# Attention with four query chunks of a head abreast, first maxima by groups of heads, and a two-part output projection

## The chip, the cores and the metric

The kernel runs on one core of a Trainium2 chip. The metric is the time of one execution on the device in microseconds (us). PE is the matrix engine (its weight loads are a row of their own, PEld), ACT the scalar engine, DVE the vector engine, POOL the general engine, SP the engine whose queue issues the DMAs (shown as SPq). The kernel before took 958.94 us, the median of three runs (958.87 to 963.58).

## The reference

Two independent sublayers over 2048 tokens of width 448, their results side by side:

```python
a = jnp.einsum("bsd,ed->bse", x, dft_hid_re)
b = jnp.einsum("bsd,ed->bse", x, dft_hid_im)
y = jnp.einsum("ts,bse->bte", dft_seq_re, a) - jnp.einsum("ts,bse->bte", dft_seq_im, b)
...
scores = jnp.einsum("bhqd,bhkd->bhqk", q, k) * scale
p = _softmax(scores, axis=-1)
o = jnp.einsum("bhqk,bhkd->bhqd", p, v)
```

Half A is a Fourier mixing by matrices. Half B is attention with 16 heads of 28 columns; q, k and v come from one product with `wqkv`, and the heads' outputs go through `wo`. Everything is float32.

## The kernel before, in words

**Number form.** A float32 product is made from rounded parts: a value is split into a rounded high part (ACT copy) and the rest (DVE or POOL subtraction), and high by high, low by high and high by low are summed in a bank of PSUM. A contraction over 448 rows so takes 11 products of 128 rows ("11" in the calls of `products`, L467).

**Filler and attention.** PE's work is of two sorts that are interleaved. The filler (mode 0): the qkv projection (L545), the hidden transforms of half A (also L545) and the two sequence transforms by classes modulo 4 (L800, 768 products of 448 columns). The sequence filler goes in 32 groups of 24 products; each group loads five blocks of DFT matrices, splits or combines them on ACT, DVE and POOL (L787, L789, L758, L763), and DVE reduces each block to a check value (L771).

The attention (L954, `unit_once`) goes in 64 units, one for each head and each chunk of 512 queries. A unit
- multiplies the chunk with the head's first 128 keys (L960), and DVE makes from this the largest score of each query: a transpose in blocks of 32 (L965), a reduction (L966), three copies that bring partition groups beside each other (L970), a reduction (L974), a transpose (L977), and a DMA of the negative maxima as an extra row into the q tile (L979);
- makes 16 score products of 128 keys by 512 queries (L988, 85 rows, "S" below), each followed by an exponential on ACT (L992);
- multiplies all 16 blocks with the values in one burst (L893, "V" below). The values of a block are 128 by 32 (28 columns, a column of ones for the sum, zeros), so a product fills a strip of 32 columns of the array; block kt goes to strip kt % 4, and so four products run side by side. The burst is mode 1: the planner counts a turn from mode 0 to it;
- copies the bank to a tile `ou` (L411 on ACT or L413 on DVE, called from `unit_out`, L897).

The four strips hold partial sums over different keys. `out_of` (L1002) adds them: for a head's four chunks it multiplies the four `ou` tiles with `fold` (L1012), a matrix of four identities, copies the result with ACT (L1015), sends the sums through DRAM to DVE for their reciprocals (L1019, L1020, L1024), spreads them over partitions by DMA (L1028), multiplies on POOL (L1031) and stores to `on_d` (L1034). The last head's four chunks go one by one.

**Output projection** (L1083, `project_out`): after the last chunk's attention, loads `on_d` back, splits it (L1110, L407) and makes 16 results of 11 products (L1129), copied out by ACT or DVE and stored (L1136).

**What sets the order.** All five queues are written out by a planner (L178 to L292) that runs when the program is built. Each task has a key (its due time), engines with assumed durations, what it depends on, and slots of tile pools; the planner walks through assumed time and gives each idle engine the ready task with the lowest key. What it writes out is fixed: on the chip each engine takes its instructions in that order, and a task whose data are late holds all that stands behind it on its engine. Attention keys run from `T_ATT` to `T_END`, filler keys to `T_FILL` (L416).

**Pools.** 16 pairs of tiles `kept` (exponentials, staging), 6 tiles for keys, 3 for queries, 4 `ou`, and 8 banks of PSUM, of which 4 are the filler's and may be borrowed.

**The guard.** Sums of exponentials outside fixed limits (`LIMIT`, `L_LEAST`) or unlike DFT blocks set a flag (L1152 and L1153), and then a second, plain pass (from L1157) does all again. The profiled execution did not run it.

## Time and profile before

| what | us |
|---|---|
| median of three runs | 958.94 |
| the profiled execution's own time | 957.11 |
| its span, first to last instruction | 954.9 |
| busy: PE, ACT, DVE, POOL | 920.9, 695.5, 515.5, 277.3 |

A line such as L988 is a line of the kernel before. In a group of instructions the columns are the line, engine, operation, tiles, shapes, count, then busy time in all and mean ns of one, then the engine's idle time just ahead of them and what ended it. Matrix products are pipelined: one takes longer than the distance to the next, so rates are read from the distance of starts or from the busy time of a whole run of them. A float32 product on a strip (values, `fold`) is recorded as two passes, so 16 products of a burst count as 32. The granted clock (PEclk) is the share of its full clock that PE was given.

### The profile page before, as it was taken

The numbers are of one execution on the slowest core, as the hardware profiler recorded it, in microseconds if no ns is written. First come the engines' busy times: TensorE is split into PE (matmuls) and PEld (weight loads), VectorE is DVE, ScalarE is ACT, GpSimd is POOL, SyncE is SP. The second block draws the span as 40 slices with busy tenths as digits, with TensorE's granted clock in tenths as the row PEclk, the third lists the DMA queues.
The fourth block names the chain that finished last, engine by engine and source line by source line (L and its number), as shares of the span: only waits on it lengthen the run. The fifth ranks groups of instructions, "written<-read, shape, count | busy, mean of one in ns | idle before, by whom it ended". The sixth has DMA issues, their size and how long they took to land. (4 is left out here: it accounts for less than half of the span.)

```text
span 954.9 us, 15430 instructions
## 1 busy us (share of the span) xinstructions
PE 920.9 (96%) x5068; PEld 597.8 (63%) x5068; DVE 515.5 (54%) x1079; ACT 695.5 (73%) x1350; POOL 277.3 (29%) x287
## 2 busy tenths in 40 slices
PE   8999999999999999997999999998899999999896
PEld 6885666665666566664665666564556566665595
DVE  6432232323225222238866776649998686766273
ACT  6167788887778887876888786777797778776541
POOL 1200010231113221115522244236583133314640
PEclk9999999999999999998999999999899999999999
DMA  8992344363335353426554455555638656545853
GB/s 280 209 173 100 114 133 142 110 203 108 121 97 162 91 164 102 154 82 191 154 158 149 117 174 142 147 188 157 213 95 240 188 167 185 170 133 149 233 177 108
DMA packets 188469, 147.54 MB, mean 155 GB/s; under 512 B 52444, under 2 KB 158428, under 8 KB 188380
## 3 DMA queue, kind: packets, MB, share of 16 engines
q1 hardware_dynamic: 188380, 146.46, 51.9%
q8 instruction: 42, 0.69, 0.3%
q14 instruction: 47, 0.39, 0.1%
HBM read 105.12 MB, written 41.03 MB: 153 GB/s over the span
## 5 line engine op out<-in xcount | busy, mean ns | idle before, releaser
L992 ACT ACTIVATE kept<-bank 128x512 f32<-128x512 f32 x1024 | 528.6, 650 | 83.3 <-PE bank L988 77.9
L988 PE MATMUL bank<-q,k 85*128 85x512 f32 x1024 | 352.0, 408 | 7.0 <-DVE ou L413 3.3
L988 PEld LDWEIGHTS bank<-q,k 85*128 85x128 f32 x1024 | 188.5, 190 | 92.7 <-ACT kept L992 29.3
L893 PE MATMUL bank<-kept,v 128*32 128x512 f32 x2048 | 233.5, 595 | 0.2 <-DVE mt L965 0.2
L800 PE MATMUL bank<-big,wlo 128*128 128x448 f32 x512 | 158.6, 380 | 8.7 <-DVE wlo L763 8.5
L893 PEld LDWEIGHTS bank<-kept,v 128*32 128x32 f32 x2048 | 61.7, 109 | 140.5 <-issue 123.6
L763 DVE TENSOR_TENSOR wlo<-wdraw,wraw 128x128 fp32r<-128x128 f32 x188 | 96.0, 549 | 52.1 <-PE bank L800 50.6
L800 PEld LDWEIGHTS bank<-big,wlo 128*128 128x128 f32 x512 | 99.0, 194 | 31.9 <-DVE wlo L763 12.0
L545 PE MATMUL bank<-big,whi 128*128 128x512 f32 (+1 forms) x324 | 109.1, 389 | 2.0 <-DVE big L407 1.4
L965 DVE STREAM_TRANSPOSE mt<-bank 128x512 f32<-128x512 f32 x64 | 45.7, 713 | 120.8 <-PE bank L960 120.6
L411 ACT ACTIVATE ou<-bank 128x512 f32<-128x512 f32 x57 | 34.0, 597 | 94.2 <-PE bank L893 94.1
L800 PE MATMUL bank<-big,whi 128*128 128x448 f32 x256 | 84.7, 373 | 0.8 <-ACT kept L992 0.4
L520 POOL TENSOR_TENSOR wlo<-wraw,whi 128x384 fp32r<-128x384 f32 x22 | 22.8, 1038 | 190.1 <-ACT whi L514 101.3
L789 POOL TENSOR_TENSOR wlo<-wraw,whi 128x512 fp32r<-128x512 f32 x21 | 33.3, 1587 | 150.9 <-PE bank L800 37.0
L545 PEld LDWEIGHTS bank<-big,whi 128*128 128x128 f32 x324 | 60.9, 189 | 21.0 <-issue 6.7
L763 POOL TENSOR_TENSOR wlo<-wdraw,wraw 128x128 fp32r<-128x128 f32 x68 | 50.5, 765 | 62.1 <-PE bank L800 60.0
L771 DVE TENSOR_REDUCE diff<-wlo 128x1 f32<-128x512 f32 x96 | 63.5, 675 | 8.1 <-POOL wlo L758 5.8
L970 DVE COPY mt<-mt 32x16 f32<-32x16 f32 x192 | 60.0, 313 | 3.7
L413 DVE COPY kept<-bank 128x448 f32<-128x448 f32 x37 | 22.3, 617 | 73.3 <-PE bank L545 52.5
L545 PE MATMUL bank<-big,wlo 128*128 128x512 f32 (+1 forms) x160 | 61.9, 388 | 0.0
L758 POOL TENSOR_TENSOR wlo<-wdraw,wraw 128x256 fp32r<-128x256 f32 x44 | 52.7, 1217 | 28.3 <-PE bank L800 26.2
L1031 POOL TENSOR_TENSOR kept<-kept 128x512 f32<-128x512 f32 (+1 forms) x19 | 25.0, 1315 | 122.9 <-DMA kept<-rd 48.2
(95 smaller groups left out, 903.3 us busy)
## 6 DMA issues: line engine op xcount, KB each, us to landing
wdraw<-wre SPq DMA_DIRECT2D x48, 256.0 KB
wdraw<-wim SPq DMA_DIRECT2D x48, 256.0 KB
kept<-abd SPq DMA_DIRECT2D x24, 448.0 KB
qkd<-wd SPq DMA_DIRECT2D x32, 256.0 KB
wraw<-wre SPq DMA_DIRECT2D x32, 256.0 KB
wraw<-wim SPq DMA_DIRECT2D x32, 256.0 KB
k<-qkd SPq DMA_DIRECT2D x64, 112.0 KB
q<-qkd SPq DMA_DIRECT2D x64, 112.0 KB
```

What stands on the lines that cost most here:

```text
L411: nc.scalar.activation(dst, src, AF.Copy)
L545: nc.tensor.matmul(o.t[:, :cols], w(), x(), start=(i == 0), stop=(i == n - 1))
L758: e.tensor_tensor(dst[:, c::2], r[:, c::2], s[:, c::2], op=op)
L763: e.tensor_tensor(dst[:, c], r[:, c], (x if turn % 2 else s)[:, c], op=ALU.subtract if plus else ALU.add)
L771: seen.append(dve(key, lambda: nc.vector.tensor_reduce(dst, f32(src.t).rearrange("p a b -> p (a b)"), axis=AX.X, op=ALU.max, apply_absolut ...
L789: b = both(key - 11.5, lambda e, hi=hi, lo=lo, same=same: e.tensor_tensor(lo.t, classes(same.t), f32(hi.t), op=ALU.subtract), 0.6, 1.25, d ...
L800: nc.tensor.matmul(o.t[:, :D], w.t[:, c], x(), start=first, stop=stop)
L893: nc.tensor.matmul(o.t[j * VW:(j + 1) * VW, :], VT[h].t[:, kt // 4, j, :], pairs[i // 2].t[:, i % 2, :], start=(kt < 4), stop=(kt >= NT - 4))
L965: r = dve(key, lambda: nc.vector.transpose(mt.t[:, :CH], o.t), 0.64, deps=[m], acq=[mt], use=[o], own=RAW_S)
L970: return lambda: nc.vector.tensor_copy(mt.t[:32, CH + i * NT:CH + (i + 1) * NT], mt.t[32 * i:32 * i + 32, CH:CH + NT])
L988: m = pe(key, lambda e, b=b, kt=kt: nc.tensor.matmul(b.t, KT[h][kt // 4].t[:KR + 1, kt % 4 * P:(kt % 4 + 1) * P], q.t[:KR + 1, :], start=T ...
L992: es.append(act(key - 20, lambda b=b, p=p: nc.scalar.activation(p.t, b.t, AF.Exp, scale=SCALE), deps=[m], use=[b, p.pair]))
```

## The change

**Four chunks abreast** (`head_once`, `four`). For heads 0 to 14 the loop over blocks of keys is outside and the four chunks inside: block 0 for chunks 0 to 3, block 1 for chunks 0 to 3, and so on. After 16 scores (four blocks, four chunks) comes a burst of 16 value products in which strip j belongs to chunk j. The strips of the one bank then hold the four chunks' finished sums over all keys; four bursts of a head accumulate into it. There is no copy to `ou` and no product with `fold`: `normal` reads the bank directly. A head now needs all four query tiles at once (8 query tiles in place of 3; 5 key tiles in place of 6). The last head keeps its chunks one by one, with `fold`.

**First maxima of groups of heads** (`tops`). For heads (0, 1), (2 to 5), (6 to 9), (10 to 13), (14, 15) one product for each chunk gives the scores of all heads of the group, by high parts alone, against each head's first 32 keys, laid out as blocks on a diagonal in a tile `kb`. The blocks of 32 make the DVE copies and the second reduction needless: transpose, reduction and transpose remain, once for each group and chunk. The result goes through DRAM (`m_d`) to the query tiles. Queries for these products are loaded extra, through a single tile `qb`.

**Output projection in two parts** (`project_late`). Nine of the eleven products of a result, over `on_d` rows 0 to 383, are filler after the sequence filler; twelve of the sixteen results are copied from their banks to tiles and wait, four stay in the filler's banks. The last two products, over the rows of the last heads, come at the end; DVE adds them to the twelve, and ACT copies the four.

**Planner.** A load marked `hold` isn't issued before the planner's filler front or its time less 60 reaches its key. The assumed flow of DMA goes from 200 to 250, the assumed durations of the sequence filler's block operations are raised, the combining loads' keys move earlier, and the ends of the key ranges move (`T_END` 860 to 783, `T_FILL` 905 to 860, `T_OUT` 860 to 807). The multiplication by reciprocals may go to DVE as well as POOL.

```diff
-NKEYS = 6
+NKEYS = 5
+NQS = 8
+NQB = 1
...
-GV = 16
+GV = 4
...
+GROUPS = ((0, 1), (2, 3, 4, 5), (6, 7, 8, 9), (10, 11, 12, 13), (14, 15))
+FIRST_KEYS = 32
+N_HELD = 12
...
-FLOW, FLOW_IN = 200.0, 400.0
+FLOW, FLOW_IN = 250.0, 400.0
...
+LAG = 60.0
...
+                    if t.hold and t.key > max(front, now - LAG):
+                        aside.append(item)
                         continue
...
+                    front = max(front, t.key) if t.mode == 0 else front
...
-    q_s = new("q", [P, CH], F32R, 3, True)
+    q_s = new("q", [P, CH], F32R, NQS, True)
+    qb_s = new("qb", [P, CH], F32R, NQB, True)
+    kb_s = new("kb", [P, P], F32R, 1)
...
-    ou_s = new("ou", [P, CH], F32, 4, True)
...
-    mt_s = new("mt", [P, CH + 6 * NT], F32, 1)
-    top_s = new("top", [32, 32], F32R, 1)
...
+    top_s = new("top", [P, 32], F32R, 2)
...
-    T_ATT, T_END, T_FILL, T_OUT = 34.0, 860.0, 905.0, 860.0
+    T_ATT, T_END, T_FILL, T_OUT = 34.0, 783.0, 860.0, 807.0
...
+                a = act(key - 12, lambda hi=hi, same=same: nc.scalar.activation(hi.t, classes(same.t), AF.Copy), 1.02,
...
-                        e, j, part, dl.t, r.t, same.t, cross.t), 0.72 if j == 2 else 0.88, 1.44 if j == 2 else 1.7,
+                        e, j, part, dl.t, r.t, same.t, cross.t), 1.1 if j == 2 else 1.45, 2.25 if j == 2 else 2.5,
...
+    def tops(g):
+        hs = GROUPS[g]
+        n = len(hs)
+        at = head_at[hs[0]] - LEAD
+        kb = kb_s.slot()
+        def keys():
+            for i, h in enumerate(hs):
+                r0 = h * 2 * DH + DH
+                nc.sync.dma_start(f32(kb.t)[i * DH:(i + 1) * DH, i * 32:(i + 1) * 32], f32(qk_d[r0:r0 + DH, 0, :FIRST_KEYS]))
+        lk = dma(at - 13, keys, hold=True, size=4, n=n, deps=[d for h in hs for d in rows_ready(h, 0, DH)], use=[kb])
+        for c in range(NC):
+            qb = qb_s.slot()
+
+            def rows(qb=qb, c=c):
+                src = bass.AP(tensor=qk_d.tensor, offset=qk_d.offset + hs[0] * 4 * DH * S + c * CH,
+                              ap=[[4 * DH * S, n], [2 * S, DH], [1, CH]])
+                nc.sync.dma_start(f32(qb.t)[:n * DH], f32(src))
+            lq = dma(at - 12 + c, rows, hold=True, size=56 * n, deps=[d for h in hs for d in rows_ready(h, c, 0)], use=[qb])
+            o, mt, top = bank_s.slot(), kept_s.slot(), top_s.slot()
+            m = pe(at + c, lambda e, o=o, qb=qb: nc.tensor.matmul(o.t[:32 * n], kb.t[:n * DH, :32 * n], qb.t[:n * DH], start=True, stop=True),
+                   deps=[lk, lq], use=[o, qb, kb])
+            key = at + c - 20
+            r = dve(key, lambda o=o, mt=mt: nc.vector.transpose(mt.t[:32 * n, 0], o.t[:32 * n]), 0.64, deps=[m], acq=[mt], use=[o], own=RAW_S)
+            r = dve(key, lambda mt=mt: nc.vector.tensor_reduce(
+                f32r(mt.t[:32 * n, 1, :NT]), mt.t[:32 * n, 0].rearrange("p (j r) -> p j r", r=32), axis=AX.X, op=ALU.max, negate=True), 0.6,
+                deps=[r], use=[mt], own=RAW_S)
+            r = dve(key, lambda mt=mt, top=top: nc.vector.transpose(
+                f32(top.t)[:32 * n], mt.t[:32 * n, 1, :NT].unsqueeze(1).to_broadcast([32 * n, 2, NT])), SMALL, deps=[r], acq=[top], use=[mt])
+            s = dma(key, lambda top=top, c=c: nc.sync.dma_start(m_d[g * NC + c][:32 * n], f32(top.t)[:32 * n]), size=4 * n, deps=[r], use=[top])
+            for i, h in enumerate(hs):
+                top_done[h, c] = s, m_d[g * NC + c][32 * i:32 * i + NT]
+
...
+    def four(h, o, tiles, es, key, kts, cs, after=None):
+
+        def emit(e):
+            for i, (kt, c) in enumerate((kt, c) for kt in kts for c in cs):
+                j = c if len(cs) > 1 else kt % 4
+                nc.tensor.matmul(o.t[j * VW:(j + 1) * VW, :], VT[h].t[:, kt // 4, kt % 4, :], tiles[i // 2].t[:, i % 2, :],
+                                 start=(kt < 4 // len(cs)), stop=(kt >= NT - 4 // len(cs)))
+        return pe(key, emit, d=0.2146 * len(kts) * len(cs), deps=[*es, *got_v[h], after], use=[*tiles, VT[h], o], mode=1)
...
+    def head_once(h):
+        t_b = head_at[h]
+        alone = h == H - 1
+        head_loads(h, [t_b - 12 + c * (4 if alone else NT) * DT for c in range(NC)], t_b - 10)
+        if alone:
+            for c in range(NC):
+                chunk_once(h, c, qs[c], got_q[c], t_b + c * NT * DT)
+            return
         last_pv = None
         for g in range(NT // GV):
+            tiles, es = [], []
+            for i in range(GV * NC):
+                kt, c = GV * g + i // NC, i % NC
+                if i % 2 == 0:
+                    tiles.append(kept_s.slot(SPARE))
+                key = t_b + (kt * NC + c) * DT
+                es.append(score(h, c, kt, qs[c], got_q[c], tiles[-1], i % 2, key))
+            last_pv = four(h, po, tiles, es, key, range(GV * g, GV * (g + 1)), range(NC), last_pv)
+        normal([(h, c) for c in range(NC)], h, po, last_pv, key + 10)
...
+    def normal(us, g, o, dep, key):
+
+        n = len(us)
+        pair = kept_s.slot()
-
-        def emit(e):
-            for i, u in enumerate(us):
-                nc.tensor.matmul(o.t[i * VW:(i + 1) * VW, :], fold, OU[u].t, start=True, stop=True)
-        m = pe(key, emit, d=0.86, deps=[ou_done[u] for u in us], use=[o, *(OU[u] for u in us)], mode=1,
-               wait=JOIN if key < T_END - 30 else 0.0)
         a = act(key - 20, lambda: nc.scalar.activation(
-            osb.t[:n * VW], o.t[:n * VW], AF.Copy, accum_out=sums[:n * VW, g:g + 1]), deps=[m], use=[o, pair])
+            osb.t[:n * VW], o.t[:n * VW], AF.Copy, accum_out=sums[:n * VW, g:g + 1]), deps=[dep], use=[o, pair])
...
-        mul = pool(key - 20, lambda: nc.gpsimd.tensor_tensor(osb.t[:n * VW], osb.t[:n * VW], sbc.t[:n * VW], op=ALU.mult),
+        mul = both(key - 20, lambda e: e.tensor_tensor(osb.t[:n * VW], osb.t[:n * VW], sbc.t[:n * VW], op=ALU.mult), 0.62, POOL_2,
...
-    combine(0, lambda g: s_at - 12 + 6 * g if g else h_at + (s_at - h_at) / QT, lambda g: x_users, lambda g, j: [h_last] if g else x_users)
+    combine(0, lambda g: s_at - 18 + 8 * g if g else h_at + (s_at - h_at) / QT, lambda g: x_users, lambda g, j: [h_last] if g else x_users)
...
+        for cc in range(2):
+            cols = slice(cc * 2 * CH, (cc + 1) * 2 * CH)
+            for k in range(3):
+                raw = kept_s.slot()
+                key = fkey(0, 0) + 2 * cc * 36 * M448 - 14 + k
+                ld = dma(key, lambda raw=raw, k=k, cols=cols: nc.sync.dma_start(
+                    raw.t.rearrange("p a b -> p (a b)"), on_d[k * P:(k + 1) * P, cols]), 512, hold=True,
+                    deps=[o_done[h, c] for h in heads_in(k) for c in (2 * cc, 2 * cc + 1)], use=[raw])
+                for i in range(2):
+                    c = 2 * cc + i
+                    free = u_last[1, c + 1] if c < 3 else z_last[1, 2, 3]
+        held = {}
+        spare = [kept_s.slot() for _ in range((N_HELD - 10 + 1) // 2)]
+        for n in range(NT):
+            c, t = divmod(n, 4)
+            cut = lambda k, c=c, t=t: (lambda: place_of(c, k)[:, t * P:(t + 1) * P])
+            seq = products(cut, lambda k, cut=cut: cut(3 + k), lambda: None, lambda k: (lambda: w.h[:, k]), lambda k: (lambda: w.l[:, k]))[:9]
+            o = fill_s.slot()
+            key = fkey(9, M448)
+            for i, (a, b) in enumerate(seq):
+                def emit(e, i=i, a=a, b=b, o=o, n=n):
+                    nc.tensor.matmul(o.t[:, :D], a(), b(), start=(i == 0), stop=(i == 8 and n < N_HELD))
+                last[0] = pe(key + i * M448, emit, d=M448, deps=[last[0], *x[c, i // 3], *(w_ready if i == 0 else ())], use=[o])
...
+        x3 = [q_s.slot() for _ in range(NC)]
+        x3_ready = []
+        for c in range(NC):
+            raw = kept_s.slot()
...
+        for n in range(NT):
+            c, t = divmod(n, 4)
+            key = T_OUT + n
+            o = bank_s.slot() if n < N_HELD else held[n]
+
+            def emit(e, n=n, o=o, xt=x3[c], t=t):
+                for i, y in enumerate((w.h, w.l)):
+                    nc.tensor.matmul(o.t[:, :D], xt.t[:, t * P:(t + 1) * P], y[:, 3], start=(i == 0 and n < N_HELD), stop=(i == 1))
+            p = pe(key, emit, n=2, d=M448, deps=[x3_ready[c], *w_ready, *([] if n < N_HELD else [last[0]])], use=[o, x3[c]])
+            if n < N_HELD:
+                s, at, put = held[n]
+                e = dve(key, lambda o=o, at=at: nc.vector.tensor_tensor(at(), at(), o.t[:, :D], op=ALU.add), 0.53, deps=[p, put], use=[o, s])
+                dma(key, lambda at=at, n=n: nc.sync.dma_start(out[n * P:(n + 1) * P, D:], at()), deps=[e], use=[s])
+            else:
+                pair = kept_s.slot()
+                e = act(key, lambda o=o, pair=pair: nc.scalar.activation(pair.t[:, 0, :D], o.t[:, :D], AF.Copy), 0.43, deps=[p], use=[o, pair])
+                dma(key, lambda pair=pair, n=n: nc.sync.dma_start(out[n * P:(n + 1) * P, D:], pair.t[:, 0, :D]), deps=[e], use=[pair])
```

More of the change, by code (lines that the diff above doesn't have):

```diff
@@ L139 @@
 class Task:
-    __slots__ = ("engs", "key", "emit", "lat", "use", "lock", "left", "then", "mode", "n", "dmas", "own", "since", "wait")
+    __slots__ = ("engs", "key", "emit", "lat", "use", "lock", "left", "then", "mode", "n", "dmas", "own", "since", "wait", "hold")
 class Schedule:
@@ L187, in run @@
         done = set()
-        landed, flow = [], FLOW_AT
+        landed, flow, front = [], FLOW_AT, 0.0
         while True:
@@ L370, in tile_kernel @@
         nc.gpsimd.memset(f32(k)[64:96, :], 1.0)
+    for k in kb_s.tiles:
+        nc.gpsimd.memset(f32(k), 0.0)
     class Half:
@@ L428, in plan @@
             head_due_b[h] = min(due[h, c][1] for c in range(NC))
-    plan(T_ATT, T_END, LEAD, 0.5)
+    head_at = [T_ATT + h * (T_END - T_ATT) / H for h in range(H)]
+    DT = (T_END - T_ATT) / (H * NC * NT)
     V_PACE = 1.0
@@ new lines, in score @@
+    def score(h, c, kt, q, got, pair, i, key):
+        b = bank_s.slot()
+        p = Half(pair, i)
+        m = pe(key, lambda e: nc.tensor.matmul(
+            b.t, KT[h][kt // 4].t[:KR + 1, kt % 4 * P:(kt % 4 + 1) * P], q.t[:KR + 1, :], start=True, stop=True),
+            deps=[*got, *got_k[h, kt // 4], before.get("rb")], use=[b, pair, q, KT[h][kt // 4]])
+        in_line("rb", m)
+        return act(key - 20, lambda: nc.scalar.activation(p.t, b.t, AF.Exp, scale=SCALE), deps=[m], use=[b, pair])
@@ L1139, in tile_kernel @@
+    for g in range(len(GROUPS)):
+        tops(g)
+    for h in range(H):
+        head_once(h)
     w_out = Weights(big[:, :8 * D])
-    project_out(w_out, load_w(w_out, lambda k: wo[:, k], g_at[1, NQ - 1, 1] - 10, after=[u_last[1, 0]]), T_OUT, [before["rb"]])
+    project_late(w_out, load_w(w_out, lambda k: wo[:, k], g_at[1, NQ - 1, 1] - 10, after=[u_last[1, 0]]))
     r = [dve(T_OUT, lambda: nc.vector.tensor_reduce(alike[:, 0], diff, axis=AX.X, op=ALU.max), 0.2, deps=seen),
```

186 lines of the change are left out of this document (97 added, 89 removed).

## The prediction

> **What bounds the kernel now.** I read the page's busy shares first, then the windows of all engines (columns: window, length, then busy us and count of PE, PEld, DVE, ACT, POOL, then granted clock, DMA share, GB/s).
>
> ```profile
> PE 920.9 (96%) x5068; PEld 597.8 (63%) x5068; DVE 515.5 (54%) x1079; ACT 695.5 (73%) x1350; POOL 277.3 (29%) x287
> ...
> 200.00:300.00 100.00, 100.00 (x568) 61.75 (x567) 27.94 (x73) 79.08 (x158) 15.00 (x18) 1.00 0.42 135
> ...
> 400.00:500.00 100.00, 93.75 (x524) 60.05 (x523) 66.10 (x122) 77.06 (x151) 35.04 (x34) 0.97 0.49 151
> 500.00:600.00 100.00, 97.91 (x568) 61.85 (x567) 70.66 (x141) 77.93 (x148) 32.72 (x31) 1.00 0.50 146
> 600.00:700.00 100.00, 93.43 (x505) 56.26 (x503) 76.50 (x133) 76.52 (x150) 51.85 (x46) 0.97 0.55 167
> 700.00:800.00 100.00, 98.15 (x562) 62.12 (x565) 80.34 (x159) 79.23 (x150) 37.08 (x31) 1.00 0.61 182
> ```
>
> PE sets the time in every stretch after the start. From 200 to 300 it never rests; from 400 on, with the sequence filler, it loses a few us in each hundred, while DVE's load goes from 28 to 80. No other engine is near its end there. So two things can shorten the kernel: fewer products, and fewer waits of PE. The waits, by who ended them (us in all, times, longest), and the slices in which the clock fell (PE alone: busy, clock, DMA share, GB/s):
>
> ```profile
> PE bank L800 <- DVE wlo L763: 8.5, 6, 5.5
> PE bank L988 <- DVE ou L413: 3.3, 1, 3.3
> PE bank L1129 <- POOL big L407: 2.0, 1, 2.0
> PE bank L988 <- DVE mt L965: 1.8, 3, 0.8
> ...
> PE bank L960 <- DMA q<-qkd: 1.8, 1, 1.8
> ...
> PE bank L1129 <- ACT big L498: 1.4, 1, 1.4
> ...
> PE bank L893 <- DVE mt L965: 0.2, 1, 0.2
> ```
>
> ```profile
> 30.00:40.00 10.00, 8.24 (x33) 0.83 0.92 266
> 40.00:50.00 10.00, 10.00 (x50) 1.00 0.98 171
> 50.00:60.00 10.00, 9.54 (x45) 1.00 0.98 166
> ...
> 440.00:450.00 10.00, 3.86 (x12) 0.79 0.92 291
> 450.00:460.00 10.00, 10.00 (x47) 0.87 0.51 146
> ...
> 660.00:670.00 10.00, 8.69 (x47) 0.89 0.21 61
> 670.00:680.00 10.00, 9.84 (x58) 0.94 0.87 279
> 680.00:690.00 10.00, 6.73 (x24) 0.83 0.45 131
> ...
> 900.00:910.00 10.00, 9.95 (x41) 0.84 0.87 245
> ```
>
> DVE ended 8.5 + 3.3 + 1.8 + 0.2 = 13.8 us of PE's waits. The clock took more: 10 x (0.21 + 0.13) = 3.4 us after the gap near 446, 10 x (0.11 + 0.06 + 0.17) = 3.4 after those near 666 and 684. A gap so costs itself and, if it is long enough, 1.7 us or more.
>
> **The change part by part.** I take counts of the changed kernel from its built instruction order.
>
> ```profile
> L988 PE MATMUL bank<-q,k 85*128 85x512 f32 x1024 | 352.0, 408 | 7.0 <-DVE ou L413 3.3 <-DVE mt L965 1.8 <-ACT kept L992 1.8
> L893 PE MATMUL bank<-kept,v 128*32 128x512 f32 x2048 | 233.5, 595 | 0.2 <-DVE mt L965 0.2
> ...
> L970 DVE COPY mt<-mt 32x16 f32<-32x16 f32 x192 | 60.0, 313 | 3.7
> L965 DVE STREAM_TRANSPOSE mt<-bank 128x512 f32<-128x512 f32 x64 | 45.7, 713 | 120.8 <-PE bank L960 120.6
> L966 DVE TENSOR_REDUCE mt<-mt 128x16 f32<-128x512 f32 x64 | 43.6, 681 | 1.7
> ...
> L411 ACT ACTIVATE ou<-bank 128x512 f32<-128x512 f32 x57 | 34.0, 597 | 94.2 <-PE bank L893 94.1
> ...
> L960 PE MATMUL bank<-q,k 84*128 84x512 f32 x64 | 26.0, 406 | 2.2 <-DMA q<-qkd 1.8 <-ACT kept L992 0.5
> ...
> L1012 PE MATMUL bank<-ou,fold 128*32 128x512 f32 x128 | 20.2, 605 | 0.1
> ...
> L974 DVE TENSOR_REDUCE mt<-mt 32x16 fp32r<-32x64 f32 x64 | 16.0, 251 | 2.2
> ...
> L977 DVE STREAM_TRANSPOSE top<-mt 32x32 f32<-32x32 f32 x64 | 12.8, 200 | 2.2
> ...
> 850.00:875.00 25.00, 2.09 (x4) 0.28 (x4) 1.00 0.46 134
> ```
>
> The last row is the window of L1012 alone.
>
> *Folds.* Four passes there, two of the last head's single folds, take 2.09. The changed kernel keeps four such folds, 4.18 us, of 20.2: **-16.0**. They stood on a full PE, so all of it counts.
>
> *First maxima.* 20 products in place of 64. A score product in a run costs the distance of starts: (0.86 - 0.39) / 2 = 0.235 us from the rows
>
> ```profile
> 882.48 0.86 PE L988 MATMUL bank<-q,k 85*128 85x512 f32 x3
> ...
> 884.27 0.39 PE L988 MATMUL bank<-q,k 85*128 85x512 f32 x1
> ...
> 921.31 11.37 PE bank L1129 x55
> ```
>
> 44 x 0.235 = **-10.3** (with the mean of one, 0.406, it would be 17.9; I take the distance, as PE is pipelined).
>
> *Unchanged.* 1024 scores, 64 bursts of 16 value products (233.5 us), 1604 filler and 176 projection products are all still there. The strips are used in turn, 0 to 3, in both; I cost four abreast at nothing.
>
> *DVE and ACT.* A unit's maxima cost DVE 0.713 + 0.681 + 3 x 0.313 + 0.251 + 0.200 = 2.8 us, 178 in all. Now 20 times 0.713 + 0.681 + 0.200, 32 in all: 146 us of DVE go, some 22 of the 66 to 80 in each hundred. ACT loses 53 of its 57 copies to `ou` (32 us); 12 multiplications go from POOL to DVE (0.68 each by the nearest row, L966's 128x512 pass: 8 us). None of this is on PE's path, but it is what stood ahead of the waits that DVE ended. I take those 13.8 and their 6.8 of clock as gone: **-20.6**, bounds 0 and -20.6. Late next is POOL, which shares the filler's blocks.
>
> *Projection.* The products only move: in the built order 118 + 30 of them, not 176 and 57 of filler, follow the last burst. The waits at its start (2.0 + 1.4, clock 10 x 0.16 = 1.6) came from splitting `wo`; that split now has 84 filler products of cover behind its release, not 36. I take half: **-2.5**, bounds 0 and -5.0. Its DMAs, copies and 12 additions lie beside products.
>
> *Start.* Head 0 now needs four query tiles and four `qb` loads before its first burst: 4 x 112 + 2 x 168 KB more, 0.80 MB, where DMA is full (0.98, 166 to 171 GB/s in the rows above): **+4.8**, bounds 0 and 12 (two clock falls and the longer way through DRAM). Behind a waiting top product or score stand the filler products, so it is PE that pays.
>
> *End.* Four stores of 224 KB leave together, not one by one: 0.69 MB at 166 to 291 GB/s, 2.4 to 4.1 us, partly beside the copies: **+2**. The last chunk's way from fold through DRAM to its two products is covered by 112 + 22 products of 11.37 / 55 = 0.207 us, 27.7 us.
>
> ```profile
> 892.74 1.04 PE L1012 MATMUL bank<-ou,fold 128*32 128x512 f32 x2
> ...
> 931.07 0.42 ACT L1110 ACTIVATE k<-kept 128x256 fp32r<-128x256 f32 x1
> ```
>
> ```profile
> L1019 SPq DMA_DIRECT2D sm<-kept x5: 612/622/624, 217.2 to 419.9; - x5
> ```
>
> ```profile
> L1031 POOL TENSOR_TENSOR kept<-kept x4: 1283/1285/1291, 226.9 to 379.7; 128x512 f32<-128x512 f32 x4
> ```
>
> Before it took 38.3 us (892.74 to 931.07), but in a queue full of filler loads; with a quiet queue (from 217.2 to 226.9) the part up to the multiplication takes 9.7. I take 0, bounds 0 and 10.6 + 1.7.
>
> *New waits.* A top product waits for the single `qb`; SP waits with it, and K, Q and matrix loads stand behind SP. The nearest row is the 1.8 us wait of L960, after which the clock fell (10 x 0.17 = 1.7): 3.5 us each. I take one, **+3.5**, bounds 0 and 20 x 3.5.
>
> On the clock the trace and a page differ. The Trainium skill, "TensorE: Matmul & The Clock Gate", Part 1, says that the clock halves after an idle window of about 3.4 us; in this trace it fell after gaps of 1.8 and 3.3 too. By the page alone only the 5.5 us gap of L800 would cost clock, and the sum would be that of rival 5.
>
> Sum: -16.0 - 10.3 - 20.6 - 2.5 + 4.8 + 2 + 3.5 = -39.1. The profiled execution took 957.1 (span 954.9 and 2.2 around it): 918.0. It lies 1.8 below the median of 958.9, so I add that: **920**.
>
> **The rivals.**
> 1. *The waits stay and change their cause.* The order is planned from assumed durations and nothing shows that POOL or DMA can't take DVE's place as releaser. Then 20.6 + 2.5 are not won: 943. Against it: DVE has the waits, and sheds about three tenths of its load.
> 2. *Every wait goes*: no loss at start, end and tops (4.8 + 2 + 3.5), the projection's other 2.5, and PE's waits for exponentials (1.8 and 0.5 in the rows of L988 and L960), ahead of which copies go: 905.
> 3. *The tops hold PE, and it gets slower.* Place: the 20 top products behind one `qb`. Price 3.5 each. Without such waits the sum is 916; 42 us are made up from 12 waiting products on, and with all 20 it is 986. Against it: only one of 64 waited so before, and outside the start DMA is half idle.
> 4. *Four abreast is not side by side.* If strips that hold the same values ran 0.6 us slower a burst (4.2 for 3.6), 64 x 0.6 = 38 us would eat the gain: 958. Against it: the strips' turn is the same.
> 5. *The clock falls only after gaps over 3.4 us.* Then the falls near 666, 684 and 900 came by themselves and stay, 3.4 + 0.8 less won: 924. This is the page's rule; the slices speak against it.
> 6. *The guard trips*, since 32 keys give lower maxima than 128, and the second pass adds its whole time, over 900. From the inputs the largest log of a sum is 54, the limit's is 82.9.
>
> **How the numbers follow.** Forecast 0.52, rivals 0.17, 0.18, 0.05, 0.03, 0.04 and 0.01. The likeliest case gives 920. The range reaches over rival 5, to rival 1 above and a little past rival 2 below: 900 to 943; outside lie rivals 3, 4 and 6 and the edges of 1 and 2, together about 0.2. A measurement of this kernel can tell 0.5% from no change. Faster: forecast and rivals 1, 2, 5, 0.91; the same: rival 4, 0.03; slower: rivals 3 and 6, 0.06.
>
> **What would show it.** Folds: 8 passes, about 4 us. Tops: 20 products. Bursts: 3.6 us each; more is rival 4. DVE's busy time near 385, ACT's near 660. Waits of PE from 430 to the attention's end that DVE ended: near none, clock 1.00; else rival 1, and its releaser names the cause. A wait at top products or the first burst of several us shows the start's or rival 3's price. After the last burst about 148 products, 31 us, with no gap ahead of the last eight. A PE that waits in many places at once would prove the forecast wrong.

## The result and the profile after

The changed kernel takes **994.67 us** (median of 4 runs, 991.42 to 997.25) against 959.74 for the kernel before beside it (958.87 to 963.58). The ratio is 1.0354 with a 95% interval of 1.031 to 1.0399: slower, where 920 was forecast. The profiled execution took 996.12, its span is 994.3. The busy shares of after:

```profile
PE 925.9 (93%) x4904; PEld 593.4 (60%) x4904; DVE 416.6 (42%) x722; ACT 660.6 (66%) x1279; POOL 244.4 (25%) x247
```

The work went as intended: 164 matrix passes fewer, 99 us less of DVE, 35 less of ACT. PE is busy for longer all the same and its share fell from 96% to 93%: it does less, more slowly, and waits more. Where, the windows show. They are cut at the start of head 7's first score product and at the end of the last score product (columns as in the prediction). Before, then after:

```profile
0.00:409.20 409.20, 403.45 (x2223) 263.12 (x2223) 137.99 (x350) 299.84 (x584) 67.67 (x90) 1.00 0.50 145
409.20:886.20 477.00, 460.24 (x2573) 288.34 (x2570) 345.95 (x662) 371.39 (x712) 184.59 (x170) 0.99 0.53 160
886.20:954.90 68.70, 57.21 (x277) 46.38 (x276) 31.54 (x68) 24.28 (x55) 24.99 (x27) 0.95 0.58 176
```

```profile
0.00:438.60 438.60, 410.08 (x2139) 264.88 (x2139) 85.98 (x184) 280.89 (x554) 54.78 (x79) 0.96 0.46 135
438.60:949.50 510.90, 478.40 (x2573) 298.11 (x2572) 317.25 (x513) 369.59 (x707) 189.25 (x168) 0.97 0.57 172
949.50:994.30 44.80, 37.46 (x195) 30.43 (x194) 13.34 (x27) 10.11 (x21) 0.37 (x1) 0.96 0.31 103
```

Heads 0 to 6 take 29.4 us more, heads 7 to 15 33.9 more, the rest 23.9 less. To split this I went through PE's products one by one in each trace. A product's distance to the next start counts as work up to the usual distance of its kind (score 0.236, 512 columns 0.233, 448 columns 0.206, bursts and folds as they run at full clock); the idle time before the next is a gap; half the time at the halved clock is clock. What is left, starts that come later than usual without a gap, is called slow starts; the trace gives no cause for them.

| us, before to after | work | gaps | clock | slow starts | sum |
|---|---|---|---|---|---|
| heads 0 to 6 | 391.3 to 380.9 | 4.4 to 27.2 | 1.7 to 14.1 | 10.5 to 15.1 | +29.3 |
| heads 7 to 15 | 436.0 to 440.1 | 16.8 to 32.5 | 6.1 to 13.2 | 17.9 to 24.9 | +33.9 |
| after the last score | 54.2 to 37.3 | 3.5 to 0.0 | 1.7 to 0.0 | 1.2 to 0.1 | -23.2 |
| all | -23.2 | +35.0 | +17.8 | +10.5 | +40.1 |

So 23 us of work were saved and 63 lost around it. What PE waited for in after (us, times, longest):

```profile
PE bank L984 <- DMA qb<-qkd: 30.3, 10, 6.1
PE bank L1000 <- ACT kept L1004: 8.6, 11, 2.0
PE bank L1000 <- DMA q<-md: 3.8, 4, 1.8
PE bank L815 <- DVE wlo L778: 3.2, 4, 0.8
PE bank L1011 <- DMA v<-vd: 2.8, 1, 2.8
```

Half of all gaps stand ahead of the product of the grouped first maxima (L984) and end when its query rows land in `qb`. Before, transfers ended 1.8 us of PE's waits. Five of these ten waits, 18.8 us, lie in heads 0 to 6, the other five, 11.5 us, in heads 7 to 15. The longest stands ahead of the very first of the 20 products, whose load is issued at 27.82 into an empty `qb`:

```profile
33.09 0.66 PE L984 MATMUL bank<-qb,kb 56*64 56x512 f32 x1 [6.11 <-DMA qb<-qkd]
```

Another wait in full, first SP's queue, then PE (start, us, what; in brackets the idle time before it), then SP's own waits for the store of the maxima from 155 to 190:

```profile
160.90 0.37 SPq L993 DMA_DIRECT2D md<-top  x1
165.81 0.24 SPq L1036 DMA_DIRECT2D q<-md  x1
166.13 0.68 SPq L981 DMA_DIRECT2D qb<-qkd  x1
...
172.58 0.23 SPq L1036 DMA_DIRECT2D q<-md  x1
173.32 0.67 SPq L981 DMA_DIRECT2D qb<-qkd  x1
```

```profile
163.39 0.50 PE L984 MATMUL bank<-qb,kb 112*128 112x512 f32 x1
...
165.60 1.83 PE L1000 MATMUL bank<-q,k 85*128 85x512 f32 x7
172.53 0.77 PE L984 MATMUL bank<-qb,kb 112*128 112x512 f32 x1 [5.09 <-DMA qb<-qkd]
173.09 1.05 PE L1000 MATMUL bank<-q,k 85*128 85x512 f32 x2
```

```profile
SPq L1036 <- DMA md<-top: 8.9, 3, 4.5
```

The product at 163.39 frees the one `qb`. The next load could go then, but SP's queue first holds the read of the stored maxima, which waits until their store (160.90) has landed, at 165.81. Only at 166.13 is the load of `qb` issued, and 6.4 us later, at 172.53, the next product can run. All that stands behind it on PE waits along. Two products then take 1.05 us instead of 0.6: the clock has fallen. It fell after shorter gaps too. Here a gap of 1.96 stands ahead of a burst that takes 5.34 us; the burst at 159.82 took 3.64:

```profile
159.82 3.64 PE L1011 MATMUL bank<-kept,v 128*32 128x512 f32 x32
```

```profile
372.53 0.51 PE L984 MATMUL bank<-qb,kb 112*128 112x512 f32 x1 [1.96 <-DMA qb<-qkd]
372.97 5.34 PE L1011 MATMUL bank<-kept,v 128*32 128x512 f32 x32
```

The windows around it, with the granted clock in the third column from the end:

```profile
369.65:373.06 3.41, 1.45 (x9) 0.58 (x11) 0.62 (x1) 2.35 (x5) 1.45 (x2) 1.00 0.60 213
373.06:376.47 3.41, 3.41 (x20) 0.87 (x24) 1.61 (x3) 0.00 (x0) 0.00 (x0) 0.50 0.40 101
376.47:379.88 3.41, 3.41 (x27) 1.49 (x19) 0.40 (x1) 1.10 (x3) 0.00 (x0) 1.00 0.23 77
```

The trace has 13 stretches at half clock, before had 6; six of the 13 begin during or just after a wait for `qb`, 34.1 us long in all, which costs 17 us at most.

### The profile page after: what moved, and what is told of

Same layout as the page of the kernel before. It is cut to its first block, busy times and chain, and to the rows that moved or that the text cites. A ratio compares the mean times of both kernels' runs of the same rounds, so it can differ in the third digit from the quotient of the medians.

```text
span 994.3 us, 14609 instructions
## 1 busy us (share of the span) xinstructions
PE 925.9 (93%) x4904; PEld 593.4 (60%) x4904; DVE 416.6 (42%) x722; ACT 660.6 (66%) x1279; POOL 244.4 (25%) x247
## 5 line engine op out<-in xcount | busy, mean ns | idle before, releaser
L1000 PE MATMUL bank<-q,k 85*128 85x512 f32 x1024 | 362.5, 416 | 16.1 <-ACT kept L1004 8.6
L1011 PE MATMUL bank<-kept,v 128*32 128x512 f32 x2048 | 238.8, 608 | 2.8 <-DMA v<-vd 2.8
L778 DVE TENSOR_TENSOR wlo<-wdraw,wraw 128x128 fp32r<-128x128 f32 x188 | 105.2, 596 | 62.6 <-PE bank L815 49.8
L560 PE MATMUL bank<-big,whi 128*128 128x512 f32 (+1 forms) x324 | 113.2, 400 | 2.4 <-ACT big L497 1.4
L535 POOL TENSOR_TENSOR wlo<-wraw,whi 128x384 fp32r<-128x384 f32 x22 | 23.2, 1055 | 305.6 <-ACT whi L529 170.6
L815 PE MATMUL bank<-big,whi 128*128 128x448 f32 x256 | 89.4, 391 | 1.3 <-DVE kept L427 1.3
L560 PEld LDWEIGHTS bank<-big,whi 128*128 128x128 f32 x324 | 62.4, 196 | 22.3 <-issue 6.3
L778 POOL TENSOR_TENSOR wlo<-wdraw,wraw 128x128 fp32r<-128x128 f32 x68 | 55.1, 836 | 76.2 <-DMA wdraw<-wre 39.4
L802 ACT ACTIVATE whi<-wraw 128x512 fp32r<-128x512 f32 x32 | 37.8, 1189 | 41.2 <-DMA wraw<-wim 19.2
L815 PEld LDWEIGHTS bank<-big,whi 128*128 128x128 f32 x256 | 50.6, 202 | 13.3 <-issue 4.2
L602 DVE TENSOR_TENSOR wd<-bank,wd 128x512 fp32r<-128x512 f32 x16 | 10.9, 686 | 98.3 <-ACT wd L601 98.3
L560 PE MATMUL bank<-wd,big 128*128 128x448 f32 x176 | 40.5, 387 | 0.1
```

The costliest lines, as they stand in the source:

```text
L535: b = sch.add(e, at, lambda g: eng[g].tensor_tensor(self.lo.t[:, :n], raw.t[:, :n], f32(self.hi.t)[:, :n], op=ALU.subtract), deps=[a], acq ...
L560: nc.tensor.matmul(o.t[:, :cols], w(), x(), start=(i == 0), stop=(i == n - 1))
L778: e.tensor_tensor(dst[:, c], r[:, c], (x if turn % 2 else s)[:, c], op=ALU.subtract if plus else ALU.add)
L802: a = act(key - 12, lambda hi=hi, same=same: nc.scalar.activation(hi.t, classes(same.t), AF.Copy), 1.02, deps=[raws[0][1]], acq=[hi], use= ...
L815: nc.tensor.matmul(o.t[:, :D], w.t[:, c], x(), start=first, stop=stop)
L1000: m = pe(key, lambda e: nc.tensor.matmul(b.t, KT[h][kt // 4].t[:KR + 1, kt % 4 * P:(kt % 4 + 1) * P], q.t[:KR + 1, :], start=True, stop=True),
```

## The experiments

Theory A: the grouped maxima hold PE, by the single `qb` and the way through DRAM and back. Rival B: the written order is at fault as a whole, and a wait taken away returns with another cause. Rival C: four chunks abreast want too much at a head's start. Rival D: the planner's new numbers (rate, durations, pacing). These letters hold for my own text; an expectation says itself what its letters stand for (in e3_owntops B is four abreast, in e4_projout C is the split projection). All but the last two kernels were timed once. One kernel's times lie up to 14 us apart (w2_lead18: 942.4 to 956.1; h2_lat and w1_lat, the same kernel: 956.7, and 952.0 to 961.2), so I read where the time goes and not only the end. Beside them the kernel before took 961.3 (e), 956.6 (f), 957.4 (g) and 959.5 (h).

**e1_extra.** `tops`, the load of `qb`, in the planner's list only:
```diff
-... size=56 * n, deps=...
+... size=56 * n, extra=3.0, deps=...
```


> Only the planner is told 3 us more for each query load of a top product; the chip's work is the same. Theory A (top products stand in PE's order ahead of loads that take 5 to 6 us through one qb tile and hold everything behind them: 30.3 us of waits and 18.7 us of clock at those places): PE's waits for qb fall from 30 to under 5 us, clock over 0.98, time 944 to 960. Rival B (the waits only show what is short anyway, so they come back at scores or sequence filler): waits of PE stay over 55 us in all, time 980 or more.

992.48 us. The waits for `qb` fell from 30.3 to 6.7, yet gaps only from 59.7 to 46.4, slow starts rose from 40.1 to 47.0. A's numbers were missed. B's time held; its 55 us of waits did not quite.

**e2_nqb2.**
```diff
-NQS = 8
-NQB = 1
+NQS = 7
+NQB = 2
```


> Two qb tiles (and 7 query tiles in place of 8, for room). Theory A: a load no longer waits for the product before it, so the second to fourth product of a group wait less; the planner still assumes short loads, so some waits stay: PE's waits for qb 5 to 15 us, time 952 to 972. Rival B: 980 or more. If one query tile less hurts, it shows as waits of scores for q.

967.58 us, as A said: 27 won by one more buffer. `qb` waits 12.0, gaps 39.4; heads 0 to 6 fell from 438.6 to 420.5. So the buffer is the larger part, and not all: the wait for the first load is still 6.2 long.

**e3_owntops.** Four abreast and the split projection stay; each chunk takes its maxima from its own rows and 128 keys, as before (`tops` gone; the product, transpose, reductions and store of the old `unit_once` in its place).

> Four abreast and the split projection stay, but every chunk makes its first maxima by itself from 128 keys, as before: 64 top products, no qb, no way through DRAM. Theory A: the 49 us of waits and clock go, 44 products of 0.235 come back, DVE is as full as before: time 945 to 970. Rival B (four abreast itself, with its new order and plan, is what loses): 980 or more.

985.02 us, which missed A's number and lies in its B's 980 or more. But heads 0 to 6 take 414.0 here; the loss is in heads 7 to 15, 521.3 (before 477.0).

**e4_projout.** `project_out` at the end in place of `project_late`.

> The output projection is one part at the end again, the rest of the change stays. Theory A: the split isn't the loss and is worth some us of filler under the attention: 996 to 1012. Rival C (the split holds the end back, by its loads and held results): under 988.

1015.34 us, above its A's 996 to 1012 and far from its C. The rest after the last score takes 94.4 instead of 44.8, heads 7 to 15 493.7 instead of 510.9, the time up to head 7 425.4 instead of 438.6: beside this plan the split wins 50 at the end and costs 30 ahead of it. The plan's pacing is made for a split, though: it costs 28 after the last score without one (h4_beforepace). Against the kernel before e4 so says nothing of the split.
```profile
425.40:919.10 493.70, 468.74 (x2495) 287.44 (x2495) 276.68 (x451) 362.60 (x695) 150.87 (x132) 0.95 0.52 156
```

**f1_latency.** e2_nqb2 and in the planner's list
```diff
-the load of qb: size=56 * n          +size=56 * n, extra=3.0
-the store of the maxima: size=4 * n  +size=4 * n, extra=1.5
-their load into q: size=2            +size=2, extra=1.5
```


> The kernel after with two buffers for the grouped q rows (as in e2_nqb2, 967.6 us) and, in the list that the planner orders by, a longer landing for the three transfers of the first maxima: 3.0 us more for the q rows, 1.5 us more for the store of the maxima and 1.5 us more for their load into q. If the waits for these three legs are what is left of the loss (12.0 us at the top products, and the head's start), 948 to 960 us with under 4 us of qb waits. If a wait that is taken away only comes back with another cause, as in e1_extra, 962 us or more with gaps still near 40 us.

966.59 us, as rival B would have it: waits for `qb` 8.7, not under 4, and 6.2 now for the maxima.

**f2_flow.** `FLOW` 250 to 200.

> The kernel after with the planner's assumed rate of transfers set back from 250 to 200, nothing else. If that assumption lets the plan start products before their rows have landed, 960 to 980 us. If it is not the cause, 985 to 1005 us, and the difference from 992 shows how far any new order of the same work scatters.

1013.49 us, above both bands. The old rate doesn't take the loss away, and another order of the same work can cost 19 us more. So a single step of that size, or smaller, can come from the order alone.

**f3_beforeplan.** The kernel before with `FLOW` 250 and the longer durations of the block splits.

> The kernel before with the planner's new figures alone (rate 250, and the longer durations of the splits of the sequence blocks), the work unchanged. If the figures make a worse order by themselves, 970 us or more. If not, 950 to 966 us.

965.55 us, 9 above before, inside the band for "not". D's numbers alone explain little.

**f4_onebyone.** Head's chunks one after the other, folds as before, grouped maxima and split projection kept (`NQS` 4, four `ou` tiles):
```diff
-        if alone:
-            for c in range(NC):
-                chunk_once(h, c, qs[c], got_q[c], t_b + c * NT * DT)
-            return
+        for c in range(NC):
+            chunk_once(h, c, qs[c], got_q[c], t_b + c * NT * DT)
+        if not alone:
+            out_of([(h, c) for c in range(NC)], h, t_b + NC * NT * DT + 10)
```


> The kernel after with the chunks of each head one after the other again (16-product bursts into one chunk, folds as before), while the first maxima stay in groups of four heads over one buffer and the projection stays split. If taking four chunks abreast is what brings the loss, because a head then needs all four q rows and maxima at its start, 945 to 970 us (the folds cost 12 more). If the grouped maxima behind one buffer bring it, 985 us or more with qb waits of 25 us or more.

995.11 us, and its first row of waits:
```profile
PE bank L984 <- DMA qb<-qkd: 29.5, 11, 5.7
```
Without four abreast the loss and the waits are those of after. Four abreast isn't needed for it: C falls as the main cause.

**g1_firstown.** e2_nqb2, with own maxima for heads 0 and 1 only (`range(1, len(GROUPS))`).

> The kernel after with two buffers for the grouped q rows (e2_nqb2, 967.6 us), and heads 0 and 1 taking their first maxima from their own q rows and 128 keys as in the kernel before, so that the first group has no store of maxima and no second trip through DRAM; the other four groups unchanged. If the start's loss (head 0 takes 113.5 us in e2_nqb2 against 100.0 before and 103.7 with own maxima everywhere) is that extra trip, 952 to 960 us. If it is the opening of head 0 with four chunks at once, 964 us or more.

961.06 us, between the two. Heads 0 to 6 414.7, from 420.5.

**g2_onebyone2.** f4_onebyone with `NQB` 2 and `NQS` 3.

> f4_onebyone (chunks one after the other, grouped maxima, split projection; 995.1 us) with two buffers for the grouped q rows (and three for q instead of four). If the single buffer is what holds the top products, 960 to 975 us, as it was worth 27 to the kernel after. If the groups cost in some other way, 985 us or more.

979.40 us, between the two: 16 won, waits for `qb` 15.5 from 29.5. The buffer is about half of the waits.

**g3_projonly.** The split projection with the planner's changes, without the other two parts: f4_onebyone with own maxima as in e3_owntops.

> The split projection alone: chunks one after the other, each chunk's first maxima from its own q rows and 128 keys, folds as before, with the planner's new figures. If the grouped maxima bring the loss, and four abreast on top of own maxima brings its own (e3_owntops, 985.0 us), this is 935 to 955 us, faster than the kernel before by what the projection gives (some 15 to 20 us). If the split projection or the planner's figures bring the loss, 970 us or more.

980.54 us, far over the 935 to 955 of A and in the other side's 970 or more. Its windows, cut as above:
```profile
0.00:408.60 408.60, 401.98 (x2205) 264.60 (x2205) 132.33 (x348) 296.74 (x579) 61.52 (x85) 1.00 0.47 138
408.60:931.40 522.80, 489.59 (x2658) 307.13 (x2657) 375.33 (x715) 386.91 (x735) 198.63 (x184) 0.95 0.55 166
```
Up to head 7 nothing is lost against before (409.2). Heads 7 to 15 take 46 more: 16.4 of work (folds and own maxima kept, filler and projection moved in from the end), 16.4 of gaps, 12.8 of clock. The releasers and, in slices of 10 us, the places where PE lost most:
```profile
PE bank L816 <- DVE wlo L779: 12.3, 12, 2.1
PE bank L1024 <- ACT kept L1028: 9.1, 5, 5.9
PE bank L816 <- DVE wlo L805: 7.3, 2, 7.0
```
```profile
470.00:480.00 10.00, 3.42 (x19) 1.62 (x12) 9.91 (x12) 5.64 (x12) 7.54 (x7) 0.81 0.67 193
...
680.00:690.00 10.00, 7.95 (x18) 5.26 (x18) 9.95 (x13) 5.89 (x12) 5.61 (x5) 0.55 0.88 286
...
900.00:910.00 10.00, 3.36 (x14) 2.48 (x14) 9.97 (x11) 4.35 (x8) 7.46 (x7) 0.81 0.47 134
```
DVE is full there, 9.9 of 10, though over the span it is busy for little more than half. These are the places where a class of the sequence starts (`combine` beside the block splits) and the end of the blocks. In the kernel before DVE was as full at such places: 9.93 from 440 to 450, 9.99 from 670 to 680.

**g4_projonly_oldplan.** g3_projonly with f3's numbers set back.

> g3_projonly with the planner's rate (200) and the durations of the sequence blocks' splits as in the kernel before. If those figures cost what they cost alone in f3_beforeplan (9 us), 928 to 945 us; if they make no order of this work better or worse by themselves, within 8 us of g3_projonly either way.

984.49 us: within 8 of g3. D's rate and durations don't explain g3.

**h3_projpace, h4_beforepace.** `T_END, T_FILL, T_OUT`: g3_projonly with 860, 905, 860; the kernel before with 783, 860, 807 and `s_at - 18 + 8 * g`.

> g3_projonly (split projection alone, 980.5 us) with the planner's pacing as in the kernel before (attention to end at 860 and the sequence products at 905 instead of 783 and 860). g3 loses nothing up to head 7 and then 45 us in heads 7 to 15. If the new pacing is what crowds VectorE and GpSimd there, 940 to 960 us. If the split projection itself does (its loads, splits and stores lie in those heads), 970 us or more.

> The kernel before with the pacing of the kernel after alone (783, 860, 807, and the first combination's keys), the work unchanged. If the pacing makes the loss of the second half, 975 us or more, with the loss in heads 7 to 15 and none before. If not, 950 to 968 us.

973.30 and 981.76 us. With the old pacing g3's heads 7 to 15 still take 516.8, inside the band for the split itself. But the stretch now holds 37 matrix passes more (2695 for 2658), and PE's waits in it fall from 33.1 to 22.2: a part of g3's loss there is the pacing. On the kernel before the new pacing does cost 22, as its number said, but not where I expected it. The window of h3, then those of h4:
```profile
416.40:933.20 516.80, 494.54 (x2695) 315.69 (x2695) 375.26 (x714) 388.85 (x740) 204.35 (x187) 0.96 0.55 167
```
```profile
400.40:883.10 482.70, 467.97 (x2577) 289.09 (x2576) 321.41 (x619) 374.29 (x716) 185.60 (x181) 0.97 0.51 154
883.10:980.00 96.90, 75.43 (x336) 60.50 (x334) 52.21 (x100) 25.62 (x54) 37.25 (x39) 0.84 0.55 175
```
Heads 7 to 15 take 5.7 more than before, the rest 28.2 more: 59 more matrix passes are put off past the attention, and the clock there is 0.84. The new pacing goes with a long end in both kernels that have the projection whole, this one and e4_projout; with it split it won nothing either (g3 980.54, h3 973.30).

**h2_lat, h1_pace.** g1_firstown with f1's three landings; and that with the pacing 820, 900, 842.

> g1_firstown (961.1 us) with the three longer landings of f1_latency in the planner's list. Those took away nearly the whole wait at head 5 and changed nothing in heads 7 to 15, so 953 to 960 us if the remaining group waits (7.5 us) go; 961 us or more if they come back elsewhere.

> h2_lat with another pacing (820, 900, 842). If the second half's loss comes with the crowding that the pacing sets, 940 to 952 us, faster than the kernel before; if it is only another order of the same work, 950 to 975 us.

956.66 and 961.48 us, both inside their bands (h1's for another order of the same work). h2_lat reaches head 7 at 410.8 (g1 414.7); the group wait at head 5 is gone. The other pacing gives nothing.

**w1_lat, w2_lead18.** h2_lat timed again; and h2_lat with `LEAD` 18 for 14.

> h2_lat again, timed against the kernel before (one look each gave 956.7 and 959.5 us): two buffers for the grouped rows, own maxima for heads 0 and 1, the three landings longer in the planner's list. If the causes named are the right ones it is no slower than before: a ratio from 0.990 to 1.002. A ratio over 1.005 would say that part of the gain of h2_lat was the one look's.

> h2_lat with the first maxima due 18 us ahead of their head instead of 14. The remaining waits before S products of heads 0, 1, 9 and 13 (some 10 us with the slow clock after them) should shrink: 948 to 955 us. If an earlier product only takes the wait along, because in the order of PE it then stands before its rows by as much as it did, 955 to 965 us.

w1_lat: 958.02 us, median of 12, ratio 0.9974 (0.9956 to 0.9992), level with before by the 0.5% bound. **w2_lead18: 946.57 us, median of 6, ratio 0.9869 (0.9833 to 0.9904)**: 1.3% faster than the kernel before, just below the 948 to 955 of its first side. Its windows, and the one wait for `qb` that is left:
```profile
0.00:409.90 409.90, 399.65 (x2142) 262.97 (x2143) 97.25 (x229) 281.50 (x554) 52.93 (x78) 0.99 0.49 143
409.90:898.80 488.90, 470.33 (x2570) 296.21 (x2569) 314.20 (x514) 369.13 (x707) 184.26 (x164) 0.98 0.59 180
898.80:945.60 46.80, 38.05 (x198) 30.98 (x196) 13.61 (x28) 10.64 (x21) 0.42 (x1) 0.95 0.29 98
```
```profile
PE bank L984 <- DMA qb<-qkd: 1.0, 1, 1.0
```
Against h2_lat heads 1, 9 and 13 are 4.2, 2.5 and 5.8 us shorter, three of the four that the expectation named; head 0 isn't. In all it has 22.3 us less work than before, and 2.9 more gaps, 4.2 more clock, 5.3 more slow starts.

The four corners, all with the split projection (us to head 7, then heads 7 to 15):

| | own maxima | grouped, one buffer | grouped, two |
|---|---|---|---|
| one chunk at a time | 408.6, 522.8 (g3) | 429.3, 517.6 (f4) | 422.5, 506.8 (g2) |
| four abreast | 414.0, 521.3 (e3) | 438.6, 510.9 (after) | 420.5, 501.0 (e2) |

Up to head 7 the grouped maxima cost 21 and 25 us with one buffer, 14 and 6.5 with two, though they are less work; four abreast cost 5 and 9, and with two buffers nothing (-2). After head 7 neither adds any. There all six take longer than the 477.0 of before, but a stretch's length mixes products that moved with time lost around them. PE's waits in heads 7 to 15 are 16 us before, 25 in e4, 32 in after, 33 in g3, 22 in h3 and 18 in w2; the granted clock is 0.99, 0.95, 0.97, 0.95, 0.96 and 0.98. So the loss there is as large without the split projection (e4), and small with it in w2, which keeps the split and the pacing of after and differs in how the first maxima are made and planned. No part of the change was shown to bring it by itself; the order has a share in it.

## Why the prediction was wrong

**Folds and first maxima** held: by distances at full clock -12.4 (forecast -16.0) and -10.4 (-10.3). For the folds I took busy time, which holds the end of the pipeline each time: 20.2 before, against 16.3 by distance. **Bursts**: by distance at full clock 228.5 us after, 229.0 before; four abreast isn't slower inside a burst, rival 4 is out. ACT's 661 is the forecast's 660. DVE's 417 is over its 385: the splits and combinations of sequence blocks on DVE go from 171 to 197 us, as more of them fell to it and many took longer (the same 188 splits 105.2 for 96.0).

**Projection and end** (-2.5 and +2) held at the end and were better: the last stretch is 23.9 shorter, 16.9 of it products that moved ahead, 6.3 waits, clock and slow starts. But I had the products move for nothing, and they moved into heads 7 to 15. Whether the move pays isn't shown: g3, which has it with the planner's changes and nothing else, is 23 us slower than the kernel before beside it.

**The step that failed first is "New waits": one of 20 at 3.5.** Ten waited, for 30.3 us, and the clock fell with six of them. The price was near, 3.0 us of wait each and up to 1.7 of clock; the count was wrong. I had named the mechanism (rival 3, "the tops hold PE", chance 0.05) and even that SP waits along, but took the count from L960, a product whose loads have three buffers. The single `qb` can't be loaded ahead: each load is issued after the product before it, at 166.13 behind a wait for stored maxima too, and so 5.1 of its 6.4 us stood on PE. The first load is another matter: its 6.1 us are not the buffer's, as two buffers leave 6.2 (e2); its product stands too early in the order. Rival 3 wanted all 20 waits for 986; ten sufficed, as the next step failed too. f4, g2, e2 and w2 show this part: the wait is there without four abreast, a second buffer takes 16 and 27 us off the time, and with own maxima for heads 0 and 1, longer landings and an earlier due time as well only 1.0 us of it is left.

**"DVE and ACT": -20.6 was not won.** Of the 13.8 us of waits that DVE ended, all in heads 7 to 15, 7.5 were left there, where I had none. Other waits came in their place: in that stretch `qb` ended 11.5 us, ACT 10.0 (2.6 before), the way of the maxima 1.8, POOL 1.7. The clock was to give back 6.8 and took 17.8 more, here and in heads 0 to 6. At a crowded place of after DVE is as full as it was before:
```profile
690.00:700.00 10.00, 8.46 (x48) 4.27 (x40) 9.81 (x16) 5.95 (x12) 2.80 (x2) 1.00 0.75 233
700.00:710.00 10.00, 8.23 (x33) 5.25 (x37) 9.96 (x15) 6.41 (x14) 6.83 (x6) 0.83 0.55 177
710.00:720.00 10.00, 7.75 (x45) 3.99 (x38) 9.90 (x12) 4.79 (x9) 6.74 (x5) 0.89 0.53 155
```
What went, the maxima's passes, lay mostly elsewhere: in heads 7 to 15 DVE lost 29 of 346 us, in heads 0 to 6, where it stood at a third, 52 of 138. I had set three tenths of an average against waits of a few crowded places. This is rival 1 (0.17), waits that stay and change their cause; e1 shows the same of the waits for `qb`.

**In no term: slow starts.** They rose by 10.5 us. No run here explains them.

**"Start": +4.8, bounds 0 and 12.** Head 2 starts 28.7 us later in the trace than before (179.4 for 150.7). The first three waits for `qb`, 14.4 us, are in this and in "New waits" both. The first group goes through DRAM once more, store and load, and four such trips follow each other over one buffer. Own maxima for two heads gave 6 back (g1), the longer landings 4 (h2), both up to head 7.

**Open.** Why waits and clock in heads 7 to 15 take so much in after and in most of its variants isn't settled. DVE is full at the places; the planner's rate and durations don't explain it (g4), the pacing explains a part (h3), the split isn't needed for it (e4), and w2 has little of it with the new rate, durations, pacing and split all kept. The loads held back by `hold` and the five key tiles are in all variants of after and were tried in none alone, nor was less DVE work in `combine`. As f2 shows, most steps between these runs are no larger than what another order can do. Nor is it shown how much of w2's 11 us over w1 is the earlier due time and how much another order of the rest.

## What to carry to other kernels

A buffer that is one deep can turn most of a load's latency into a wait of the consumer (here 5.1 of 6.4 us, with DMA under half busy); so price a new load by buffer depth and what stands ahead of its issue, not by a load that is prefetched, and count how many of its consumers will stand behind it. Put relief and crowd side by side stretch by stretch: an engine at 54% over the span can be full at the very places where the waits are. When an order is written ahead, taking one wait away shows only if the order knows the true landing time: here the gain came with the second buffer, own maxima for two heads, the longer landings and an earlier due time together.

## What the runs showed of the hardware

**A store and its read back through DRAM.** 16 KB of maxima stored at 160.90 can be read from 165.81, 4.9 us, and a strided load of 224 KB then takes 6.4 to its use, with DMA at 0.28 to 0.44. The Trainium skill, "DMA: Bandwidth & Descriptors", Anatomy of one DMA, gives about 2.0 us of fixed cost plus bytes at 436 GB/s, for another way of issuing. By it the load would take an estimated 2.5 us; this case's rows are two and a half times that.

**The clock falls in steps of 3.41 us.** After a single gap of 1.96 us a burst took 1.70 longer (5.34 for 3.64), half of one step at half clock. All 13 stretches at half clock of after start on one grid of 3.41 us, and all but the last, which the end cuts off, last one or two steps (3.41 or 6.83). The step ahead of the fall at 373.06 had PE busy for 1.45 of its 3.41 us; so the clock can fall without an idle gap as long as a step. Which share of a step must be idle isn't shown. The Trainium skill, "TensorE: Matmul & The Clock Gate", Part 1, names an idle window of about 3.4 us: the trace agrees with its length, and the prediction's doubt that PE must idle through all of it stands.

**DVE is slowed beside GpSimd (POOL), but only in some forms.** In g3_projonly, from 200 to 330 (GpSimd busy for 28.50 of 130) and from 660 to 710 (30.05 of 50), the same passes took:
```profile
L1006 DVE TENSOR_REDUCE kept<-kept 128x16 f32<-128x512 f32 x10 | 6.8, 683 | 0.4
...
L1010 DVE COPY kept<-kept 32x16 f32<-32x16 f32 x30 | 5.7, 190 | 0.6
```
```profile
L779 DVE TENSOR_TENSOR wlo<-wdraw,wraw 128x128 fp32r<-128x128 f32 x20 | 16.8, 897 | 0.0
...
L1010 DVE COPY kept<-kept 32x16 f32<-32x16 f32 x9 | 6.5, 717 | 0.2
...
L1006 DVE TENSOR_REDUCE kept<-kept 128x16 f32<-128x512 f32 x3 | 2.1, 686 | 0.1
```
Small copies went from 190 to 717 ns and the splits take 897, against a mean of 547 over this kernel; the reductions stay at 683 and 686. The Trainium skill, "SBUF — State Buffer", SBUF: two separate sides, says that DVE and GpSimd take turns at one pair of ports, a whole instruction at a time, when DVE runs in a mode that uses two ports, as a float32 copy within SBUF does, or reads two operands from SBUF while GpSimd reads SBUF as well. The rows agree. By this reading DVE's 9.9 of 10 in those slices is partly waiting for GpSimd; no run here takes GpSimd's part away.
